# A state-space block and a bilinear feed-forward layer on one core: factor products in one visit, decays inside pair 1's wait, pairs 2, 3 and 5 reordered

## The chip, the core and the metric

The kernel runs on one core of one Trainium2 chip. A core has TensorE (PE, matrix products into the accumulation memory PSUM; PEld is its weight load), VectorE (DVE), ScalarE (ACT), GpSimd (POOL) and SyncE (SP, which only issues transfers); 16 DMA engines move data between memory and the core. ACT and POOL issue some transfers as well. The metric is the device time of one execution in microseconds; lower is better. The figure for a kernel is the median of several executions.

## The reference

Inputs: x (4 batches, 8 heads, 768 positions, 32 columns), a (4, 8, 768), B and C (4, 8, 768, 16), and three weight matrices. The first half is a recurrence with decays, computed in chunks; the second a feed-forward layer without a nonlinearity, in which two projections are multiplied.

```python
for c in range(nc):                               # chunks of 32 positions in the reference
    cum = np.cumsum(log_a[chunk])
    L = np.exp(cum[i] - cum[j]) * (i >= j)
    y_intra = (C_i . B_j * L) @ x                 # masked scores times x
    y_inter = (C_i @ state) * np.exp(cum)
    y = y_intra + y_inter
    state = exp(sum(la)) * state + sum_j B_j x_j * exp(cum[-1] - cum[j])
X = y, as 3072 tokens x 256
out = ((X @ w_a) * (X @ w_b)) @ w_out             # 256 -> 1536, 1536 -> 256, float32
```

## The kernel before, in words

**Tiles.** The kernel works in blocks of 128 positions: NBLK = 6 blocks, and in each two pairs (NBP = 2) of batches, so 12 pairs, p = 0 to 11; pair p belongs to block p // 2. Inside a pair the two batches are indexed bt. Pairs 0 to 3 (p < P0) hold positions in an even/odd layout and have their B and C turned by TensorE (`transposes`); pairs 4 to 11 have them turned by a transposing transfer from SP (`turn`). All products take float16 operands, except the factor and decay products, which are float32.

**Decays.** Running products Pr of a within each block come from VectorE (`scan`, L225), rmid is one over the product at position 63, selr spreads that over heads. A factor product (`factors_mm`, L240) turns Pr into fC, one factor for each position and head; fB is its reciprocal (`fb`). For block 1 it is written as four small products (L260), for blocks 2 to 5 as two half-width ones each (L248); each logical product appears as two records in the profile. B times fB and C times fC (`scale_bc`) give bm and cm. Three small POOL steps make hr, hs and hsx, the decay from one block to the next spread over batches, and one product (gps, L815) with the head indicator spreads it over partitions; ACT copies it to G.

**A pair.** `scores(p)` multiplies C by B into four PSUM banks SC. `mask` multiplies each of the four by the causal mask: VectorE does it directly from PSUM; with `by_pool=True` ACT first copies to tmp and POOL multiplies. `scale_x` makes X16 from x. `pv(p)` (products L433, with the state's part L477 from block 1 on, and the new state's sums L460 in `ds_mm`) makes the output of the recurrence, which ACT and VectorE evacuate to X2T, the input of the feed-forward layer. `state_sums` (VectorE) and `state_spread` (POOL) carry the state on to the pair of the next block. From block 2 on a block's two pairs share `outputs`, called by `group`.

**Feed-forward.** For pairs 0 to 3, a unit (p, k2) is 4 products with Wa, 4 with Wb (L601, 256 columns each), an ACT copy of the first result (asb, L615) and a VectorE product of the two (hk, L622); six units make a pair's hidden layer, and `out_half(p, bt)` multiplies it by Wo in 12 products (L637), which ACT evacuates (`out_store`). From block 2 on, `bunit` (L667) and `bout` (L694) do the same for a whole block. The first halves of Wa and Wb (k2 = 0, 1, 2) are loaded early, the second halves (k2 = 3, 4, 5) by `load_w(1)` from POOL.

**Order.** The schedule is manual: each engine runs its instructions in the order in which the Python text issues them, and a program adds semaphore waits. So the text is the order of every queue, SP's and POOL's too, and a POOL transfer keeps POOL busy while it is issued. The feed-forward has four PSUM banks; `bank` hands them out in the order of the string BANKS, and a product that gets a bank waits until that bank's last reader is done. Warm-up products (`warmup`, L218) multiply zeros and are read by nobody.

The lines around the change, in the order of the text: the front with pair 1 (L754 to L818), the units of pairs 0 and 1 (L836 to L842), pair 2 (L850 to L858), pair 3 (L912 to L930), pairs 4 and 5 (L931 to L951), and the last stores (L707).

Of the kernel before, what the change touches and what calls it, by code (L numbers as in the profile page):

```python
# [14 lines left out]
ALU = mybir.AluOpType  # L15
# [4 lines left out]
YS = 16.0  # L20

BANKS = (
    "01231031203120312031230123012301203120321032103120312031203213012301203210321032130120312"
    "0312032130213021302132013201320132013201320132013021302130213021302130213021302130213021"
)


# [1 line left out]
def kernel(  # L29
# [13 lines left out]
    nc = tc.nc  # L43
# [83 lines left out]
    def bank(name):  # L127
        return psf.tile([128, 512], f32, name=name, tag=f"ff{next(banks)}")
# [89 lines left out]
    def warmup(n, bank, cols=512):  # L218
        for _ in range(n):
            nc.tensor.matmul(  # L220
                bank[:, 0:cols], warm[:, 0:128], warm[:, 0:cols], start=True, stop=True, skip_group_check=True
            )
# [462 lines left out]
    def bout(blk, c, parts=1):  # L685
        bt, j = divmod(c, NBP)
        hk = st[("FF", blk)]["hk"]
        rows = out[(2 * j + bt) * S + blk * Q :][0:Q]
        w = d_model // parts
        for part in range(parts):  # L690
            o_ps = bank("ops")
            cs = slice(part * w, part * w + w)
            for k in range(NK):
                nc.tensor.matmul(  # L694
                    o_ps[:, 0:w],
                    hk[:, k, c * Q : (c + 1) * Q],
                    Wo[:, k, cs],
                    start=(k == 0),
                    stop=(k == NK - 1),
                    skip_group_check=True,  # L700
                )
            o_sb = outp.tile([128, d_model], f32, name="osb", tag="osb")
            if parts > 1 and part == 0:
                nc.vector.tensor_scalar(o_sb[:, 0:w], o_ps[:, 0:w], 1.0 / (YS * YS), None, ALU.mult)
            else:
                nc.scalar.activation(out=o_sb[:, 0:w], in_=o_ps[:, 0:w], func=AF.Copy, scale=1.0 / (YS * YS))  # L706
            (nc.sync, nc.scalar)[part].dma_start(rows[:, cs], o_sb[:, 0:w])  # L707

    def loads_bc(p):
        if p < NP:  # L710
# [11 lines left out]
    def go(*items):  # L722
        for p, k2 in items:
            unit(p, k2)()
# [47 lines left out]
    scan(5, NBLK)  # L772
    over_mid(1, NBLK)
    sel_over_mid(1, NBLK, nc.vector)
    warmup(2, tcp)
    aps = [unit_mm(0, 0, Wa), unit_mm(0, 1, Wa)]
    asb = [evac_a(aps[0])]
    scores(1)
    mask(product(1, 3), by_pool=True)
    aps.append(unit_mm(0, 2, Wa))  # L780
    asb.append(evac_a(aps[1]))
    asb.append(evac_a(aps[2]))
    fps = bank("fps")
    factors(1, 3, fps)
    scale_x(1, nc.scalar)
    for m in range(3):
        mask(product(1, m))
# [1 line left out]
    for bt in range(2):  # L789
        load1(nc.gpsimd, 2, 1, bt)  # L790
    load_wo(0)
    nc.gpsimd.tensor_copy(maskbd, headm.unsqueeze(2).broadcast_to((128, H, D)))
    nc.gpsimd.tensor_tensor(out=hr, in0=Pr[:, 0:NG, Q - 1], in1=rmid[:, 0:NG], op=ALU.mult)
    nc.gpsimd.tensor_tensor(out=hs, in0=hr, in1=Pr[:, 1:NBLK, 63], op=ALU.mult)
    nc.gpsimd.tensor_tensor(
        out=hsx,
        in0=hs.unsqueeze(1).broadcast_to((BH, nb, NG)),
        in1=selb.rearrange("p (b g) -> p b g", b=nb),
        op=ALU.mult,
    )  # L800
    load_wo(1)
    tiles(3)
    for bt in range(2):
# [1 line left out]
    times(0, 0, bps[0], asb[0])  # L805
    pv(1, DS=(0, SC[:2]), split=True)
    ds_mm(0, 64, SC[:2])
    for k2 in range(1, 3):
        times(0, k2, bps[k2], asb[k2])
    fb(1)  # L810
    scale_bc(2, 0, nc.gpsimd)
    scale_bc(2, 1, nc.gpsimd)
    go((1, 0), (1, 1), (1, 2))
    gps = bank("gps")
    nc.tensor.matmul(  # L815
        gps[:, 0 : nb * NG], indm, hsx.rearrange("p b g -> p (b g)"), start=True, stop=True, skip_group_check=True
    )
    nc.scalar.copy(G.rearrange("p b g -> p (b g)"), gps[:, 0 : nb * NG])  # L818
    factors(3, NBLK, bank("fps"))
    state_sums(0)  # L820
    state_sums(1)
    state_spread(0)
# [10 lines left out]
        load1(nc.sync, 3, 1, bt)  # L833
    loads_x(3, nc.sync)
    loads_bc(4)
    go((0, 3), (0, 4), (1, 3), (0, 5))  # L836
    transposes(2, apart=True)
    go((1, 4))
    h = unit(1, 5)
# [6 lines left out]
    scale_x(2, nc.scalar)  # L846
    scale_bc(3, 0, nc.gpsimd)
    scale_bc(3, 1, nc.gpsimd)
    scale_x(3, nc.gpsimd)
    loads_bc(5)  # L850
    o = [bank("ops"), bank("ops")]
    out_mm(0, 0, o[0], range(6))
    out_mm(0, 1, o[1], range(6))
    out_mm(0, 0, o[0], range(6, NK))
    out_store(0, 0, o[0])
    pull(2)
    pv(2, split=True)
    out_mm(0, 1, o[1], range(6, NK))  # L858
    out_store(0, 1, o[1])
    h = unit(2, 0, lambda: transposes(3, apart=True))  # L860
    state_sums(2)
    fb(2)
# [47 lines left out]

    scores(3)
    prep(4, (2,))  # L912
    loads_bc(6)
    prep(5)
    loads_x(4, nc.sync)
# [1 line left out]
    loads_bc(7)  # L917
    mask(product(3, 0))
    h()
    for m in range(1, 4):  # L920
        mask(product(3, m))
    out_half(1, 0)
    out_half(1, 1)
    go((2, 2))
    pull(3)
    pv(3)
    state_sums(3)
    fb(3)
    state_spread(3)
    go((2, 3), (2, 4), (2, 5))  # L930
    scores(4)  # L931
    mask(product(4, 3), by_pool=True, by_token=True)
    prep(6)
    masked(4, (0, 1, 2))
    out_half(2, 0)
    o_ps = bank("ops")
    out_mm(2, 1, o_ps, range(NK))
    out_store(2, 1, o_ps)
    go((3, 0))
    scores(5)  # L940
    mask(product(5, 3), by_pool=True, by_token=True)
    prep_x(4)
# [1 line left out]
    prep(7)  # L944
    loads_x(7, nc.sync)
    loads_bc(8)
    masked(5, (0, 1, 2), *pu(3, 1, 2, 3))
    go((3, 4))
    scale_x(5, nc.scalar)
    go((3, 5))  # L950
    group(2)  # L951
# [92 lines left out]
```

## Time and profile before

| | |
|---|---|
| median of 3 runs | 124.44 us (124.07 to 124.65) |
| profiled execution | 123.91 us |
| its span, first to last instruction | 122.2 us |
| granted TensorE clock | 1.000 |
| TensorE busy | 117.1 us, 96% of the span |
| VectorE, ScalarE, GpSimd busy | 85.9, 71.4, 61.9 us |
| memory read, written | 11.13, 3.15 MB |

The profile describes one execution. Its page gives busy times and shares, the span in 40 slices, the chain of work that ended last, and groups of instructions by source line; the trace can also be asked for a timeline, for who waited for whom, and for one tile's or one line's instructions. A name such as `aps<-X2T,Wa` says that the tile aps is written from X2T and Wa; "128*128 128x256" that 128 rows and 128 columns of the array are used and 128 x 256 elements written; "x4" that four neighbouring instructions are merged. A bracket at a line's end gives the idle time before it and what ended that. Matmuls are pipelined, so two neighbours overlap in the timeline, and their cost is the distance between their starts.

### The profile page before, as it was taken

How to read it: one execution, taken by the hardware profiler on the slowest of the kernel's cores; microseconds unless marked ns; L12 is line 12 of the kernel's file. 1: busy time of each engine (PE TensorE's matmuls, PEld its weight loads, DVE VectorE, ACT ScalarE, POOL GpSimd, SP SyncE). 2: the span in 40 equal slices, each digit the busy share in tenths (PEclk: the TensorE clock that was granted, in tenths of full speed). 3: DMA queues.
4: the chain of work that ended last, by engine and by line, in shares of the span. 5: the costliest groups of instructions: out<-in, count | busy, mean ns of one | idle time of the engine just before them, and what ended most of it. 6: DMA issues, size and time to landing. Idle time of an engine off the chain costs nothing.

```text
span 122.2 us, 3713 instructions
## 1 busy us (share of the span) xinstructions
PE 117.1 (96%) x1455; PEld 80.1 (66%) x1455; DVE 85.9 (70%) x163; ACT 71.4 (58%) x141; POOL 61.9 (51%) x107
## 2 busy tenths in 40 slices
PE   5999999999999999999999999999999999999990
PEld 2446789978898898644476464766465684645880
DVE  1877897795969599499984999667799435748000
ACT  0367756866466477887668637745645737575230
POOL 7999998966953876099921993147400000000000
PEclk9999999999999999999999999999999999999999
DMA  3999999998969999799789854879501012010131
GB/s 64 165 167 240 152 215 155 218 143 83 95 95 131 150 104 155 76 134 148 55 143 128 200 187 127 96 102 160 161 0 51 16 45 68 0 48 0 43 117 55
DMA packets 66737, 13.73 MB, mean 112 GB/s; under 512 B 61616, under 2 KB 66384, under 8 KB 66720
## 3 DMA queue, kind: packets, MB, share of 16 engines
q1 hardware_dynamic: 62592, 9.53, 49.8%
q0 software_dynamic: 2128, 3.61, 16.8%
q10 hardware_dynamic: 2000, 0.36, 1.6%
q8 instruction: 11, 0.18, 0.7%
q14 instruction: 6, 0.05, 0.1%
HBM read 11.13 MB, written 3.15 MB: 117 GB/s over the span
## 4 chain that ended last, share of the span: by engine, by line
PE 93%; ACT 1%; issue 1%; POOL 1%; DVE 1%; POOLq 0%
PE ops L694 18%; PE aps L667 17%; PE bps L667 17%; PE aps L601 9%; PE ops L637 9%; PE bps L601 9%; PE SC L220 3%; PE SC L358 2%; PE SC L419 2%; PE SC L373 1%; PE SC L433 1%; PE SC L508 1%; PE fps L260 1%; POOL bm L304 1%; ACT bt L337 1%
## 5 line engine op out<-in xcount | busy, mean ns | idle before, releaser
L615 ACT COPY asb<-aps 128x512 f32<-128x512 f32 x72 | 42.0, 586 | 14.3 <-PE aps L667 9.6
L679 DVE TENSOR_TENSOR hkb<-bps,asb 128x512 f16<-128x512 f32 x48 | 32.4, 689 | 12.6 <-ACT asb L615 11.4
L667 PE MATMUL aps<-XB,Wa 128*128 128x512 f16 x96 | 28.6, 379 | 0.0
L667 PE MATMUL bps<-XB,Wb 128*128 128x512 f16 x96 | 28.5, 379 | 0.0
L694 PE MATMUL ops<-Wo,hkb 128*128 128x256 f16 (+1 forms) x204 | 22.5, 267 | 0.0
L694 PEld LDWEIGHTS <-hkb 128*128 128x128 f16 x204 | 18.5, 98 | 3.1
L413 DVE TENSOR_TENSOR t<-SC,causal_q 128x512 f16<-128x512 f32 x27 | 17.3, 682 | 3.3 <-PE SC L358 3.3
L622 DVE TENSOR_TENSOR hk<-bps,asb 128x512 f16<-128x512 f32 x24 | 16.2, 684 | 4.1 <-ACT asb L615 3.7
L667 PEld LDWEIGHTS <-Wb 128*128 128x128 f16 x96 | 9.9, 103 | 10.9
L667 PEld LDWEIGHTS <-Wa 128*128 128x128 f16 x96 | 9.7, 103 | 9.1 <-issue 0.2
L601 PE MATMUL aps<-X2T,Wa 128*128 128x256 f16 x96 | 14.3, 274 | 0.2 <-DVE X2T L493 0.2
L706 ACT ACTIVATE osb<-ops 128x256 f32<-128x256 f32 (+1 forms) x16 | 6.0, 377 | 14.3 <-PE ops L694 14.2
L601 PE MATMUL bps<-X2T,Wb 128*128 128x256 f16 x96 | 14.1, 273 | 0.0
L411 POOL TENSOR_TENSOR t<-tmp,causal_q 128x512 f16<-128x512 f32 x5 | 5.8, 1161 | 11.7 <-ACT tmp L410 11.6
L289 POOL TENSOR_SCALAR x<-xn 128x512 f16<-128x512 f32 x7 | 10.4, 1490 | 2.1 <-DMA xn<-in_x_dram 1.8
L637 PE MATMUL ops<-Wo,hk 128*128 128x256 f16 x96 | 11.3, 273 | 0.0
L601 PEld LDWEIGHTS <-Wa 128*128 128x128 f16 x96 | 9.4, 103 | 1.3 <-DVE X2T L493 0.3
L601 PEld LDWEIGHTS <-Wb 128*128 128x128 f16 x96 | 9.8, 103 | 0.6
L637 PEld LDWEIGHTS <-hk 128*128 128x128 f16 x96 | 9.0, 98 | 1.3
L413 DVE TENSOR_TENSOR t<-SC,causal 128x512 f16<-128x512 f32 x13 | 8.2, 684 | 0.9 <-PE SC L373 0.8
L304 POOL TENSOR_TENSOR bm<-bn,fB 128x256 f16<-128x256 f32 x11 | 7.1, 642 | 2.5 <-DMA bn<-in_B_dram 1.7
L296 POOL TENSOR_TENSOR planes<-cn,fC 128x256 f16<-128x256 f32 x8 | 5.0, 620 | 4.7 <-DMA cn<-in_C_dram 4.5
(94 smaller groups left out, 117.0 us busy)
## 6 DMA issues: line engine op xcount, KB each, us to landing
out_dram<-osb SPq DMA_DIRECT2D x23, 128.0 KB, 1.8
xn<-in_x_dram SPq DMA_DIRECT2D x7, 256.0 KB, 4.2
cn<-in_C_dram SPq DMA_DIRECT2D x8, 128.0 KB, 3.9
bn<-in_B_dram SPq DMA_DIRECT2D x8, 128.0 KB, 4.5
Wa<-in_moe_w_a_dram POOLq DMA_DIRECT2D x2, 384.0 KB, 5.9
Wb<-in_moe_w_b_dram POOLq DMA_DIRECT2D x2, 384.0 KB, 7.3
Wo<-in_moe_w_out_dram POOLq DMA_DIRECT2D x2, 384.0 KB, 6.7
xn<-in_x_dram POOLq DMA_DIRECT2D x4, 128.0 KB, 6.5
```

Source lines behind the costliest of these rows:

```text
L289: eng.tensor_scalar(xo, xi, XS, None, ALU.mult)
L304: eng.tensor_tensor(out=m_, in0=raw, in1=(f[:, blk, :, bp] if factor is None else factor).unsqueeze(3).broadcast_to((128, 2, H, N)), op=AL ...
L411: nc.gpsimd.tensor_tensor(out=o_, in0=tmp, in1=c_, op=ALU.mult)
L413: nc.vector.tensor_tensor(out=o_, in0=i_, in1=c_, op=ALU.mult)
L601: nc.tensor.matmul(ps[:, kk * 2 * Q : (kk + 1) * 2 * Q], W[k // 6][:, f, k % 6 // 3 * 384 : (k % 6 // 3 + 1) * 384].rearrange("p (c kk) -> ...
L615: (nc.vector.tensor_copy if on_dve else nc.scalar.copy)(asb, a_ps)
L622: nc.vector.tensor_tensor(out=s["hk"][:, 2 * k2 : 2 * k2 + 2, :].rearrange("p k q -> p (k q)"), in0=b_ps, in1=asb, op=ALU.mult)
L637: nc.tensor.matmul(o_ps[:, 0:d_model], hk[:, k, bt * Q : (bt + 1) * Q], Wo[:, k, :], start=(k == 0), stop=(k == NK - 1), skip_group_check= ...
L667: nc.tensor.matmul(t_, W[k // 6][:, f, k % 6 // 3 * 384 : (k % 6 // 3 + 1) * 384].rearrange("p (c kk) -> p kk c", kk=3)[:, k % 3], XB[:, b ...
L679: return lambda: nc.vector.tensor_tensor(out=s["hk"][:, k], in0=ps[1], in1=asb, op=ALU.mult)
L694: nc.tensor.matmul(o_ps[:, 0:w], hk[:, k, c * Q : (c + 1) * Q], Wo[:, k, cs], start=(k == 0), stop=(k == NK - 1), skip_group_check=True,)
L706: nc.scalar.activation(out=o_sb[:, 0:w], in_=o_ps[:, 0:w], func=AF.Copy, scale=1.0 / (YS * YS))
```

## The change

- Two warm-up products ahead of unit (0, 0) are dropped.
- The POOL steps hr, hs and hsx are issued ahead of pair 1's pooled mask, instead of after the first Wo load and maskbd.
- `factors` makes blocks 1 to 5 in one visit ahead of pair 0's Wb products (24 records and one copy), instead of blocks 1 and 2 there and blocks 3 to 5 after unit (1, 2).
- gps moves from after unit (1, 2) to after pair 1's `pv` and pair 0's `ds_mm`, and becomes two products of 64 columns of the array each.
- Units (0, 3), (0, 4), (1, 3): the three Wa halves with their copies first, then the three Wb halves.
- Pair 2: the second half of `out_half(0, 1)` and the first 6 products of `out_half(1, 0)` go ahead of `pv(2)`, the other 6 behind it.
- Pair 3: its fourth mask goes by ACT and POOL instead of VectorE; `scale_x(3)` goes from POOL to ACT; unit (2, 3) comes ahead of `pv(3)`; `out_half(1, 0)` is no longer here.
- Pairs 4 and 5: units (3, 1) and (3, 2) come ahead of `scores(5)`, and `out_half(2, 1)` behind pair 5's masks.
- The store of the last column group of block 4 is issued by POOL instead of SP.
- BANKS is another string, one shorter.

```diff
@@ -20,8 +20,8 @@
 BANKS = (
-    "01231031203120312031230123012301203120321032103120312031203213012301203210321032130120312"
...
+    "0123102310231012301230123012031230123013201320130213021302130213021320312031203102132013"
...
@@ -704,7 +704,8 @@
                 nc.vector.tensor_scalar(o_sb[:, 0:w], o_ps[:, 0:w], 1.0 / (YS * YS), None, ALU.mult)
             else:
                 nc.scalar.activation(out=o_sb[:, 0:w], in_=o_ps[:, 0:w], func=AF.Copy, scale=1.0 / (YS * YS))
-            (nc.sync, nc.scalar)[part].dma_start(rows[:, cs], o_sb[:, 0:w])
+            eng = nc.gpsimd if (blk, c) == (NBLK - 2, 3) else (nc.sync, nc.scalar)[part]
+            eng.dma_start(rows[:, cs], o_sb[:, 0:w])
 
     def loads_bc(p):
         if p < NP:
@@ -772,16 +773,23 @@
     scan(5, NBLK)
     over_mid(1, NBLK)
     sel_over_mid(1, NBLK, nc.vector)
-    warmup(2, tcp)
     aps = [unit_mm(0, 0, Wa), unit_mm(0, 1, Wa)]
     asb = [evac_a(aps[0])]
+    nc.gpsimd.tensor_tensor(out=hr, in0=Pr[:, 0:NG, Q - 1], in1=rmid[:, 0:NG], op=ALU.mult)
+    nc.gpsimd.tensor_tensor(out=hs, in0=hr, in1=Pr[:, 1:NBLK, 63], op=ALU.mult)
+    nc.gpsimd.tensor_tensor(
+        out=hsx,
+        in0=hs.unsqueeze(1).broadcast_to((BH, nb, NG)),
+        in1=selb.rearrange("p (b g) -> p b g", b=nb),
+        op=ALU.mult,
+    )
     scores(1)
     mask(product(1, 3), by_pool=True)
     aps.append(unit_mm(0, 2, Wa))
     asb.append(evac_a(aps[1]))
     asb.append(evac_a(aps[2]))
     fps = bank("fps")
-    factors(1, 3, fps)
+    factors(1, NBLK, fps)
     scale_x(1, nc.scalar)
     for m in range(3):
         mask(product(1, m))
@@ -790,14 +798,6 @@
         load1(nc.gpsimd, 2, 1, bt)
     load_wo(0)
     nc.gpsimd.tensor_copy(maskbd, headm.unsqueeze(2).broadcast_to((128, H, D)))
-    nc.gpsimd.tensor_tensor(out=hr, in0=Pr[:, 0:NG, Q - 1], in1=rmid[:, 0:NG], op=ALU.mult)
-    nc.gpsimd.tensor_tensor(out=hs, in0=hr, in1=Pr[:, 1:NBLK, 63], op=ALU.mult)
-    nc.gpsimd.tensor_tensor(
-        out=hsx,
-        in0=hs.unsqueeze(1).broadcast_to((BH, nb, NG)),
-        in1=selb.rearrange("p (b g) -> p b g", b=nb),
-        op=ALU.mult,
-    )
     load_wo(1)
     tiles(3)
     for bt in range(2):
@@ -805,18 +805,24 @@
     times(0, 0, bps[0], asb[0])
     pv(1, DS=(0, SC[:2]), split=True)
     ds_mm(0, 64, SC[:2])
+    gps = bank("gps")
+    for c0 in (0, 64):
+        nc.tensor.matmul(
+            gps[c0 : c0 + 64, 0 : nb * NG],
+            indm[:, c0 : c0 + 64],
+            hsx.rearrange("p b g -> p (b g)"),
+            start=True,
+            stop=True,
+            skip_group_check=True,
+            tile_position=(0, c0),
+        )
+    nc.scalar.copy(G.rearrange("p b g -> p (b g)"), gps[:, 0 : nb * NG])
     for k2 in range(1, 3):
         times(0, k2, bps[k2], asb[k2])
     fb(1)
     scale_bc(2, 0, nc.gpsimd)
     scale_bc(2, 1, nc.gpsimd)
     go((1, 0), (1, 1), (1, 2))
-    gps = bank("gps")
-    nc.tensor.matmul(
-        gps[:, 0 : nb * NG], indm, hsx.rearrange("p b g -> p (b g)"), start=True, stop=True, skip_group_check=True
-    )
-    nc.scalar.copy(G.rearrange("p b g -> p (b g)"), gps[:, 0 : nb * NG])
-    factors(3, NBLK, bank("fps"))
     state_sums(0)
     state_sums(1)
     state_spread(0)
@@ -833,7 +839,11 @@
         load1(nc.sync, 3, 1, bt)
     loads_x(3, nc.sync)
     loads_bc(4)
-    go((0, 3), (0, 4), (1, 3), (0, 5))
+    us = [(0, 3), (0, 4), (1, 3)]
+    asb = [evac_a(unit_mm(p, k2, Wa)) for p, k2 in us]
+    for (p, k2), a_ in zip(us, asb):
+        times(p, k2, unit_mm(p, k2, Wb), a_)
+    go((0, 5))
     transposes(2, apart=True)
     go((1, 4))
     h = unit(1, 5)
@@ -846,17 +856,20 @@
     scale_x(2, nc.scalar)
     scale_bc(3, 0, nc.gpsimd)
     scale_bc(3, 1, nc.gpsimd)
-    scale_x(3, nc.gpsimd)
     loads_bc(5)
     o = [bank("ops"), bank("ops")]
     out_mm(0, 0, o[0], range(6))
     out_mm(0, 1, o[1], range(6))
     out_mm(0, 0, o[0], range(6, NK))
     out_store(0, 0, o[0])
+    out_mm(0, 1, o[1], range(6, NK))
+    out_store(0, 1, o[1])
+    o_ps = bank("ops")
+    out_mm(1, 0, o_ps, range(6))
     pull(2)
     pv(2, split=True)
-    out_mm(0, 1, o[1], range(6, NK))
-    out_store(0, 1, o[1])
+    out_mm(1, 0, o_ps, range(6, NK))
+    out_store(1, 0, o_ps)
     h = unit(2, 0, lambda: transposes(3, apart=True))
     state_sums(2)
     fb(2)
@@ -910,6 +923,7 @@
 
     scores(3)
     prep(4, (2,))
+    mask(product(3, 3), by_pool=True)
     loads_bc(6)
     prep(5)
     loads_x(4, nc.sync)
@@ -917,26 +931,23 @@
     loads_bc(7)
     mask(product(3, 0))
     h()
-    for m in range(1, 4):
+    for m in range(1, 3):
         mask(product(3, m))
-    out_half(1, 0)
+    scale_x(3, nc.scalar)
     out_half(1, 1)
-    go((2, 2))
+    go((2, 2), (2, 3))
     pull(3)
     pv(3)
     state_sums(3)
     fb(3)
     state_spread(3)
-    go((2, 3), (2, 4), (2, 5))
+    go((2, 4), (2, 5))
     scores(4)
     mask(product(4, 3), by_pool=True, by_token=True)
     prep(6)
     masked(4, (0, 1, 2))
     out_half(2, 0)
-    o_ps = bank("ops")
-    out_mm(2, 1, o_ps, range(NK))
-    out_store(2, 1, o_ps)
-    go((3, 0))
+    go((3, 0), (3, 1), (3, 2))
     scores(5)
     mask(product(5, 3), by_pool=True, by_token=True)
     prep_x(4)
@@ -944,8 +955,9 @@
     prep(7)
     loads_x(7, nc.sync)
     loads_bc(8)
-    masked(5, (0, 1, 2), *pu(3, 1, 2, 3))
-    go((3, 4))
+    masked(5, (0, 1, 2))
+    out_half(2, 1)
+    go((3, 3), (3, 4))
     scale_x(5, nc.scalar)
     go((3, 5))
     group(2)
```

More of the change, by code (lines that the diff above doesn't have):

```diff
@@ L22 @@
 BANKS = (
-    "01231031203120312031230123012301203120321032103120312031203213012301203210321032130120312"
-    "0312032130213021302132013201320132013201320132013021302130213021302130213021302130213021"
+    "0123102310231012301230123012031230123013201320130213021302130213021320312031203102132013"
+    "2013203102310231023103210321032103210321032103210231023102310231023102310231023102310231"
 )
```

## The prediction

> **What bounds the kernel now.** I read the page first (who is busy, at what clock, what the chain consists of), then TensorE's waits, then the timeline of 8 to 20 us and of 24 to 48 us, where the edits lie.
>
> ```profile
> PE 117.1 (96%) x1455; PEld 80.1 (66%) x1455; DVE 85.9 (70%) x163; ACT 71.4 (58%) x141; POOL 61.9 (51%) x107
> ...
> PEclk9999999999999999999999999999999999999999
> ...
> PE 93%; ACT 1%; issue 1%; POOL 1%; DVE 1%; POOLq 0%
> ```
>
> TensorE (PE) is the chain, at full clock in every slice. The waits view of PE has one row for the start and these two:
>
> ```profile
> PE SC L373 <- ACT bt L337: 0.2, 1, 0.2
> PE aps L601 <- DVE X2T L493: 0.2, 1, 0.2
> ```
>
> So after 16 us PE waits for nobody that the view shows: a change wins only by taking instructions or switches out of PE's queue, and loses wherever it makes PE wait. The timeline of the edited stretch (start, duration, engine, line, count):
>
> ```profile
> 10.49 0.59 PE L220 MATMUL tc<-warm 128*128 128x512 f16 x2
> ...
> 10.92 1.04 PE L601 MATMUL aps<-X2T,Wa 128*128 128x256 f16 x8
> ...
> 11.60 1.44 POOL L148 DMA_DIRECT2D bn<-in_B_dram  x2
> ...
> 12.79 0.42 PE L260 MATMUL fps<-selr,Pr 32*64 32x16 f32 x8
> ...
> 13.06 0.28 PE L248 MATMUL fps<-selr,Pr 32*64 32x32 f32 x4
> 13.11 1.16 POOL L411 TENSOR_TENSOR t<-tmp,causal 128x512 f16<-128x512 f32 x1
> 13.27 1.49 PE L601 MATMUL bps<-X2T,Wb 128*128 128x256 f16 x12
> ...
> 14.70 0.42 PE L433 MATMUL SC<-t,x 64*32 64x128 f16 x32
> ...
> 14.95 0.59 PE L460 MATMUL SC<-x,bm 64*32 64x64 f16 x32
> ...
> 15.22 0.42 DVE L493 TENSOR_SCALAR X2T<-SC 128x256 f16<-128x256 f32 x1 [0.28 <-PE SC L433]
> ...
> 15.70 0.62 PE L601 MATMUL aps<-X2T,Wa 128*128 128x256 f16 x4 [0.16 <-DVE X2T L493]
> ...
> 16.69 0.22 POOL L793 TENSOR_TENSOR hr<-Pr,rmid 32x5 f32<-32x5 f32 x1
> ...
> 17.50 0.79 POOL L170 DMA_DIRECT2D Wo<-in_moe_w_out_dram  x1
> ...
> 17.91 0.60 PE L601 MATMUL bps<-X2T,Wb 128*128 128x256 f16 x4
> ...
> 18.44 0.39 PE L815 MATMUL gps<-hsx,c 32*128 32x20 f32 x2
> ...
> 18.76 0.54 PE L248 MATMUL fps<-selr,Pr 32*64 32x32 f32 x12
> ...
> 19.23 0.62 PE L601 MATMUL aps<-X2T,Wa 128*128 128x256 f16 x4
> ```
>
> Durations of products overlap, so I price PE by starts: two 512-column warm-ups take 10.92 - 10.49 = 0.43; eight 256-column products 0.87, so 0.109 each and 0.44 for a half unit of four.
>
> **The change part by part.**
>
> *Two warm-ups gone.* The products behind them read X2T, whose last evacuation ends at 10.46, and can start at 10.49: everything on PE is 0.43 earlier. Scores of pair 1 move from 11.88 to 11.45; their first half needs bt's first copy (ends 11.16) and ct (11.14), so nothing new is late there.
>
> *All factors in one visit.* Twelve more small records go behind the first twelve. Twelve cost 0.47 (18.76 to 19.23), four cost 0.21 (13.06 to 13.27), switch back included: 0.033 each by the difference, and 0.029 if the switch costs what it does elsewhere (0.15); I take 0.37 for twelve. Their inputs are there: VectorE's last scan, reciprocal and selr end by 11.99. The Wb products start at 13.27 - 0.43 + 0.37 = 13.21, pair 1's pv could start at 14.64. One copy of 160 columns replaces two on ScalarE (0.24 each); it costs nothing on the path, since x(1) behind it was done at 14.65 and ScalarE's row starts earlier.
>
> *The three small POOL steps ahead of pair 1's pooled mask.* POOL is in the two bn issues until 11.60 + 1.44 = 13.04, later than everything that hr reads. The three steps took 17.50 - 16.69 = 0.81 with their hand-overs. The mask therefore starts at 13.85 and ends at 15.01; with 0.04 for the hand-over PE sees it at 15.05. Heads 6 and 7 need it, the last 12 of pv's 32 products; in the trace these began at about 14.70 + 20/32 x 0.25 = 14.86. So pv ends 0.19 later than before: the mask that was off the path (done at 14.27) becomes the gate, and takes back all that the warm-ups gave. Queued behind it on POOL: two cn issues and the first Wo issue 0.8 later. cn's landing is behind Wb's in the same queue anyway; Wo's two landed 6.6 to 6.8 after issue, so at 23.0 and 24.3, and the output products that read the halves come at 24.5 and 25.8: covered. The second xn issue already waited for Wb until 19.32, which absorbs the shift, so bm(2) stays at 20.02.
>
> *The decays' product (gps) in pair 1's wait.* The ds products end at 15.54 in the trace and PE then waits for X2T, which is read at 15.70; without that wait it would have gone on at about 15.48 (at 28.07 the output products start 0.06 before the modelled end of such a ds group). So 0.22 is free. The two half-width products, two passes each, are of the form 32*64: about 0.06 as two pairs of factor records. Bounds: nothing if the 0.22 hides all, the whole 0.32 of the old place (18.44 to 18.76) if nothing is hidden. Between 64*32 and 32*64 there may be a switch; the nearest row is gps to factors, 0.13 behind the second gps start plus its own 0.06, so 0.19. 0.19 + 0.06 - 0.22 leaves 0.03, and I take 0.05. The Trainium skill (TensorEngine Tiling (Array Packing), Key Properties) says that a change of tiling mode, not of tile, drains the array; this case's rows agree (0.20 between starts on entering a tiled form, 0.15 on leaving). It speaks against this place, since the old one had gps and factors share one way in and out; by it the sum below would be 0.05 smaller than for a gps wholly hidden.
>
> *The second visit gone.* The next half unit after 17.91 would start at 18.35; it starts at 19.23. That removes 0.88.
>
> *Three Wa half units, then three Wb.* The same 24 products. By the steps so far the first starts at 19.23 - 0.88 + 0.19 + 0.05 = 18.59; the first that reads the second half of Wb comes at 19.90 instead of 19.03. SP's load that waits for this Wb goes out at 19.09, so the old order would have gained a wait. New neighbours: the first Wb product takes the bank of (1,2)'s, free at 19.42 + 0.24 = 19.66; (0,5) at 21.21 takes that of the third Wa, which ScalarE copies at 0.59 each by about 20.95. Both hold by a quarter of a us: nothing, at most 0.2 if the copies run late. G's copy is ahead of the asb copies in a gap of 0.75 on ScalarE: nothing.
>
> *Pair 2.* Twelve output products move ahead of pv(2): 1.31 more cover. The 18 products before pv(2) at 25.16 should end at 27.13, and the next start is 27.25, when VectorE's masks end (27.19): 0.10 gained. The same 12 are missing later, so order alone moves scores(3) by +1.31, pv(3) by 0.87, scores(4) by 0.
>
> *Pair 3.* Mask (3,3) leaves VectorE (0.63) for ScalarE (0.59) and POOL (1.16); x(3) leaves POOL (1.50, and a 1.04 wait before it) for ScalarE (0.63). Cover between scores and pv falls from 32 products to 28, 0.44 less, but VectorE has 0.63 less: nothing. POOL: pair 4's steps can start when cn(4) lands, so by about 29.8 instead of 30.95, and end with gU(2) near 33.0; the mask takes it to 34.2, and planes(5) and bm(5) (0.62 each) end at 35.4, where the trace has 35.44. So pair 5's transposing load keeps its time.
>
> *Pair 5.* Scores(5) come four products later in the order. In the trace the load was issued at 36.25 and took 5.4 to land, so 41.65; scores(5) move from 42.17 to 42.17 + 0.44 - 0.74 = 41.87. Covered by 0.2. Masks then have 36 instead of 40 products before the group, and are first in VectorE's queue: nothing. x(4) ends on POOL near 45.7, read at 46.5.
>
> *One store on POOL.* SP issued each late store as it came and has nothing to queue behind. POOL's loads landed 3 to 8 us after issue against SP's 1.7; issued at 113.3 it lands at 121.4 at worst, with the last store at 120.1 then; nearest, with DMA idle 90%, are the short ones. Nothing, bound +1.3.
>
> **Sum** against the profiled execution, 123.91 us (span 122.2 and 1.7 around it): -0.88 + 0.19 + 0.05 - 0.10 = -0.74, so 123.17. That execution lies 0.53 under the median of the three runs, 124.44 (124.07 to 124.65); against the median the forecast is 123.70, 0.6% faster. About 0.5% is what a measurement of this kernel tells from no change.
>
> **Rivals.**
> 1. The POOL mask is no gate (its three steps run quicker between other work). Then pv starts at 14.64 and gps hides: -0.06 - 0.88 - 0.10 = -1.04, 123.4. For: the steps work on 5 to 20 columns. Against: their 0.81 in the trace.
> 2. Given back in small waits: gps at 0.32 and 0.2 for a bank in the Wa-Wb run: -0.74 + 0.27 + 0.2 = -0.27, 124.2, no change. For: margins of 0.2. Against: ScalarE and VectorE keep pace at the same rate as before.
> 3. Slower, by one mechanism: the transposing load of pair 5 lands late, because POOL has mask (3,3) ahead of pair 5's steps, SP waits for POOL, and x(4) queues behind. PE then waits one for one past 41.87. With the whole 1.16 added it lands at 42.8 and 0.9 comes back: 124.6. It is slower by over 0.5% from a landing 1.6 late (43.3) on; at 1.8 late, 125.3. For: this landing was the longest of the eight (2.8 to 5.4). Against: POOL sheds x(3) first, and bm(5) had stood idle 0.78.
>
> **How the numbers follow.** Forecast 0.47, rival 1 0.12, rival 2 0.24, rival 3 0.17. Four fifths of the forecast lie beyond 0.5% (under 123.82): faster 0.38 + 0.12 = 0.50; same 0.09 + 0.24 = 0.33; slower 0.17. The range goes from rival 1 less half the runs' spread (0.29), 123.1, to 124.9, just past rival 3's milder case; the forecast's own is 123.4 to 124.0.
>
> **What would show it.** Right: no warm-up at 10.5, one factor visit with 24 records, POOL's mask ending near 15.0 with PE's pv held for POOL, gps between ds and (1,0), Wa of (0,3) at about 18.6, scores(4) near 37.5, all later stages 0.7 earlier. Wrong: PE waits for POOL much before or after 15.05, a wait for ScalarE or VectorE at 19 to 24, or PE held at scores(5).

## The result and the profile after

The changed kernel takes 123.0 us (median of four, 122.51 to 123.35) against 124.25 (124.02 to 124.65) for the kernel before on the same chip: ratio 0.9885 [0.9849, 0.9921]. Two later comparisons gave 0.989 [0.9846, 0.9934] and 0.9908 [0.9887, 0.9928]. The forecast was 123.70 us, 0.6% faster, with a range of 123.1 to 124.9. The direction was right; the gain is nearly twice the forecast, and the median lies just under the range.

The profiled execution took 122.51 us, its span 120.81 (before: 123.91 and 122.21), so the 1.40 us lies wholly inside the span. Busy times and the chain, from the page of the changed kernel:

```profile
PE 115.7 (96%) x1455; PEld 79.4 (66%) x1455; DVE 85.2 (71%) x162; ACT 72.1 (60%) x142; POOL 62.3 (52%) x108
...
PEclk9999999999999999999999999999999999999999
...
PE 89%; DMA 4%; POOL 3%; issue 0%; ACT 0%; POOLq 0%
```

TensorE still carries the chain at full clock, but a transfer has entered it with 4%: the load of Wa's first half. The waits view of PE has three rows for the changed kernel, all of them before 12 us.

The timeline of the changed kernel where most of the edits lie:

```profile
10.58 0.78 PEld L601 LDWEIGHTS <-Wa 128*128 128x128 f16 x8 [0.31 <-DMA Wa<-in_moe_w_a_dram]
10.58 1.06 PE L601 MATMUL aps<-X2T,Wa 128*128 128x256 f16 x8
...
12.48 0.42 PE L260 MATMUL fps<-selr,Pr 32*64 32x16 f32 x8
...
12.74 0.63 PE L248 MATMUL fps<-selr,Pr 32*64 32x32 f32 x16
12.78 0.25 POOL L778 TENSOR_TENSOR hr<-Pr,rmid 32x5 f32<-32x5 f32 x1
...
13.31 1.49 PE L601 MATMUL bps<-X2T,Wb 128*128 128x256 f16 x12
...
13.55 1.16 POOL L411 TENSOR_TENSOR t<-tmp,causal 128x512 f16<-128x512 f32 x1
...
14.03 0.63 ACT L287 ACTIVATE x<-xn 128x512 f16<-128x512 f32 x1
...
14.73 0.42 PE L433 MATMUL SC<-t,x 64*32 64x128 f16 x32
...
15.55 0.29 PE L810 MATMUL gps<-hsx,c 32*64 32x20 f32 x4
...
15.77 0.62 PE L601 MATMUL aps<-X2T,Wa 128*128 128x256 f16 x4
...
17.98 0.60 PE L601 MATMUL bps<-X2T,Wb 128*128 128x256 f16 x4
...
18.41 1.47 PE L601 MATMUL aps<-X2T,Wa 128*128 128x256 f16 x12
```

Set against the rows of before, this is where the time went, by starts on PE, and in the last three rows by landings and ends:

| mark | before | after | moved |
|---|---|---|---|
| first Wa product | 10.92 | 10.58 | -0.34 |
| first factor record | 12.79 | 12.48 | -0.31 |
| first Wb product | 13.27 | 13.31 | +0.04 |
| pair 1's pv | 14.70 | 14.73 | +0.03 |
| unit (1, 0) | 15.70 | 15.77 | +0.07 |
| unit (0, 3) | 19.23 | 18.41 | -0.82 |
| transposes of pair 2 | 22.74 | 21.91 | -0.83 |
| scores(4) | 38.24 | 37.28 | -0.96 |
| last product | 118.70 | 117.75 | -0.95 |
| last landing of a transfer | 120.85 | 119.90 | -0.95 |
| SP's last wait is over | 121.30 | 119.91 | -1.39 |
| end of the span | 122.21 | 120.81 | -1.40 |

Two gains, then: 0.95 us on TensorE, all of it made by 38 us, and 0.44 us after the last landing, where no engine computes. SP's waits after 117 us, first before and then after, show the second (waited-for, then us in total, times, longest):

```profile
SPq L1039 <- DMA out_dram<-osb: 1.8, 1, 1.8
```

```profile
SPq L1051 <- DMA out_dram<-osb: 1.4, 3, 0.7
```

Before, SP sat 1.8 us on one transfer and then still had a list to go through. After, it is done 0.01 us behind the last landing.

### The profile page after: what moved, and what is told of

Read it like the earlier page. It is cut to its first block, busy times and chain, and to the rows that moved or that the text cites. A ratio compares the mean times of both kernels' runs of the same rounds, so it can differ in the third digit from the quotient of the medians.

```text
span 120.8 us, 3711 instructions
## 1 busy us (share of the span) xinstructions
PE 115.7 (96%) x1455; PEld 79.4 (66%) x1455; DVE 85.2 (71%) x162; ACT 72.1 (60%) x142; POOL 62.3 (52%) x108
## 4 chain that ended last, share of the span: by engine, by line
PE 89%; DMA 4%; POOL 3%; issue 0%; ACT 0%; POOLq 0%
PE ops L694 18%; PE aps L667 18%; PE bps L667 17%; PE ops L637 9%; PE aps L601 9%; PE bps L601 9%; DMA Wa<-in_moe_w_a_dram 4%; PE SC L358 2%; PE SC L419 2%; POOL cn L148 1%; PE SC L373 1%; PE SC L433 1%; PE SC L508 1%; POOL bn L148 1%; POOL causal L208 1%; PE SC L460 1%
## 5 line engine op out<-in xcount | busy, mean ns | idle before, releaser
L615 ACT COPY asb<-aps 128x512 f32<-128x512 f32 x72 | 41.8, 586 | 14.1 <-PE aps L667 9.7
L708 POOL DMA_DIRECT2D out_dram<-osb x1 | 0.6, 639 | 27.3 <-ACT osb L706 27.3
L289 POOL TENSOR_SCALAR x<-xn 128x512 f16<-128x512 f32 x6 | 8.9, 1489 | 1.0 <-DMA xn<-in_x_dram 0.7
```

The lines of the kernel that those rows point to most:

```text
L289: eng.tensor_scalar(xo, xi, XS, None, ALU.mult)
```

## The experiments

Two theories were to be told apart from rivals. **A (the end):** at the end SP waits for the semaphores of all transfers one after the other, in a fixed order, and the one store that POOL issues shifts which semaphore the last store reports to; the 0.44 us is the rest of the list behind it. Its rival: the store's own landing or the queue's load counts. **L (the front):** pair 1's pv starts when x(1) or the Wb products are ready, x(1) is set by the landing of xn(1), and so the warm-ups and the factors ahead of it are cheap either way. Its rivals: the warm-ups' 0.43 us or POOL's mask count, as the prediction had it.

### The end of the program

**One store back on SP**, the rest of the change kept:

```diff
-            eng = nc.gpsimd if (blk, c) == (NBLK - 2, 3) else (nc.sync, nc.scalar)[part]
-            eng.dma_start(rows[:, cs], o_sb[:, 0:w])
+            (nc.sync, nc.scalar)[part].dma_start(rows[:, cs], o_sb[:, 0:w])
```

> The changed kernel with one part undone: block 4's last store goes out on SP again. Theory A (the end of the program): SP waits for the semaphores of all transfers one after the other, about 0.06 us each, and the SP and ACT transfers take eight semaphores in turn. In the kernel before, the last store's semaphore was waited for second, so seven waits stood behind the last landing (120.85 to 121.32 in its trace); in the changed kernel it is the last one waited for (119.90 to 119.94). With the store on SP the turn falls back: about 0.4 us comes back between the last landing and the end, TensorE unchanged, 123.4 us against the changed kernel's 123.0. Theory B (the prediction's: that store costs and brings nothing): no difference, the whole gain lies on TensorE, 123.0.

The ratio to the kernel before was 0.997 [0.9941, 1.0] (124.18 against 124.45): slower than both theories had it. Its trace shows two things. The tail is back: last landing 121.01, SP's last wait over at 121.45, 0.44 us. And its front was late for reasons that the store cannot have: Wa landed at 11.05 (10.54 in the changed kernel's profile), xn(1) at 14.61 (13.94), and the transposes of pair 2 waited 0.46 us for another late tile. So this run confirmed A's size in the trace and left the time open; it was repeated below.

**The kernel before with that one store on POOL**, and with **another store of the same block** instead:

```diff
+            eng = nc.gpsimd if (blk, c) == (NBLK - 2, 3) else (nc.sync, nc.scalar)[part]
```

```diff
+            eng = nc.gpsimd if (blk, c) == (NBLK - 2, 0) else (nc.sync, nc.scalar)[part]
```

> The kernel before with that one store on POOL and nothing else. Theory A: TensorE unchanged, the end 0.4 us sooner after the last landing, 123.85 against 124.25. Theory B: no difference, 124.25.

> The kernel before with another store on POOL: block 4's first column group, some 20 us before the end, and the last one on SP as before. Theory A (only the turn of the semaphores counts): the same 0.4 us as with the late store, 123.85. A rival to it (the late store itself is relieved, SP's queue at the end being one shorter): no difference, 124.25.

0.9966 [0.9935, 0.9997] and 0.997 [0.9944, 0.9996]: 0.34% and 0.30% of 124.45, about 0.4 us each, with nothing else changed in the kernel; each interval only just leaves out no change. Which of the two stores goes to POOL does not matter. SP's waits after 117 us show the same row in both:

```profile
SPq L1040 <- DMA out_dram<-osb: 1.4, 3, 0.7
```

**All stores of block 4 on POOL**, in the kernel before:

```diff
+            eng = nc.gpsimd if blk == NBLK - 2 else (nc.sync, nc.scalar)[part]
```

> The kernel before with all four stores of block 4 on POOL. Theory A: the turn moves by four places, so three waits stand behind the last landing, about 0.2 us between the last landing and SP's last wait, where the kernel before has 0.45 and one store on POOL has 0.04. The rival (fewer SP stores near the end are better): less than with one store on POOL.

One execution, 123.64 us; the tail is 0.20 us, between the two others. This is the run that best separates A from its rival, because more stores off SP did not make the end shorter still. The trace gives the semaphore of every transfer and SP's last waits, nine of them, issued by the line that calls the kernel, about 0.06 us each when nothing is left to wait for. Transfers from SP and ACT take eight semaphores in turn, waited for at the 2nd to the 9th place; POOL's take others. One transfer less in that turn puts the last store one place back in it, from the 2nd round to the 9th; four less put it at the 6th:

| kernel | last landing | SP's last wait over | between | last store's place in the nine waits |
|---|---|---|---|---|
| before | 120.85 | 121.30 | 0.45 | 2nd, seven behind it |
| changed, store on SP | 121.01 | 121.45 | 0.44 | 2nd |
| before, four stores on POOL | 120.83 | 121.03 | 0.20 | 6th, three behind it |
| before, one store on POOL | 121.72 | 121.73 | 0.01 | 9th, none behind it |
| changed | 119.90 | 119.91 | 0.01 | 9th |

**Store back on SP, timed again** beside the changed kernel:

> The changed kernel with block 4's last store on SP, once more. If the store is worth only the end of the program: 0.35% slower than the changed kernel beside it, whatever the landings. If the first figure (0.3% faster than before) was right as it stood: 0.8% slower than the changed kernel, and there would be something that the traces have not shown.

> The changed kernel beside the next three, on one chip: 1.1% faster than before, as in two comparisons; if landings are late on this chip (first Wa after 11.0, second half of xn(1) after 14.4), less, about 0.7%, since its front waits for them where the kernel before waits less.

0.9944 [0.9919, 0.997] (123.41 us) without the store on POOL, 0.9908 [0.9887, 0.9928] (122.93 us) with it: 0.36%, 0.45 us, though the two intervals overlap a little; the trace has the same 0.44 (120.55 to 120.99). The changed kernel's 0.92% lies between the two figures expected of it; in its trace the landings were early (Wa 10.18, xn(1) 13.63), so it does not show what late ones cost. In the profiled execution with the store on SP Wa came late (11.22), and PE shows that it waits one for one:

```profile
11.27 1.06 PE L601 MATMUL aps<-X2T,Wa 128*128 128x256 f16 x8 [0.74 <-DMA Wa<-in_moe_w_a_dram]
```

A is shown by its size in every trace above and by the in-between case, which it orders rightly. The times agree with it in three comparisons (0.30 to 0.36%), none of them far clear of its noise; the first comparison of the store on SP gave 0.85% and does not fit by time. A kernel further below that moves two loads from POOL to ACT adds to it: two transfers more in the turn, the last store at the 3rd place, 0.39 us behind its landing.

### The front

**The two warm-ups put back**, then once more with more executions:

```diff
+    warmup(2, tcp)
     aps = [unit_mm(0, 0, Wa), unit_mm(0, 1, Wa)]
```

> The changed kernel with the two warm-ups back. Theory L (landings): pair 1's pv cannot start sooner than 0.76 after the second half of xn(1) has landed, because ACT scales x(1) first (seven traces so far: landings from 13.71 to 14.81, pv 0.76 to 0.82 behind where it waits for x), nor sooner than 1.42 after the first Wb product. The warm-ups take 0.43 of a time in which TensorE otherwise waits for Wa, so the first Wa product starts at the later of 10.7 and Wa's landing, and pv at the later of 14.85 and the landing of xn(1) plus 0.76: 0 to 0.13 behind the changed kernel. The prediction's theory (the pooled mask is the gate, the warm-ups' 0.43 is taken back whole): no difference. A theory in which the warm-ups' 0.43 counts: 0.43 later.

> The changed kernel with the two warm-ups back, once more. Theory L (the front is set by the landings of Wa and xn(1)): 0 to 0.1% slower than the changed kernel, not to be told apart. If the warm-ups' 0.43 us counted: 0.35% slower.

The first gave 123.13 us in one execution, with pv at 14.84, 0.11 later than in the changed kernel, and a wait of 0.5 us that neither theory has, in pair 0's state sums (PE at L460, put down to "issue"). Its cause stays open. The second gave 0.9894 [0.9875, 0.9912] (122.82 us), not to be told from the changed kernel beside it (0.9908). In its trace Wa's products started at 10.85, as late as the warm-ups make them, and unit (0, 3) at 18.61, 0.2 later than in the changed kernel (18.41, and 18.42 beside it). Dropping the warm-ups is worth between nothing and 0.2 us, not 0.43.

**POOL's three small steps issued twice**, so that the pooled mask of pair 1 comes later still:

```diff
         op=ALU.mult,
     )
+    nc.gpsimd.tensor_tensor(out=hr, in0=Pr[:, 0:NG, Q - 1], in1=rmid[:, 0:NG], op=ALU.mult)
+    nc.gpsimd.tensor_tensor(out=hs, in0=hr, in1=Pr[:, 1:NBLK, 63], op=ALU.mult)
+    nc.gpsimd.tensor_tensor(
+        out=hsx,
...
+    )
     scores(1)
```

> The changed kernel with the three small POOL steps done twice ahead of the pooled mask, the second time over the first with the same values: 0.8 us more on POOL. In the changed kernel's trace the mask ends at 14.71 and its heads' products come at 14.89, or later where pv waits for x(1), so it has 0.15 of room or more. The mask ends at about 15.5 now: pv of pair 1 starts as before, but ends 0.4 to 0.65 later, and so does everything behind it. If the mask were already the gate: 0.8 later. If it had much room: nothing.

123.96 us in one execution, with a late front. Its timeline:

```profile
14.80 1.15 POOL L411 TENSOR_TENSOR t<-tmp,causal 128x512 f16<-128x512 f32 x1
...
15.03 0.63 ACT L287 ACTIVATE x<-xn 128x512 f16<-128x512 f32 x1 [0.75 <-DMA xn<-in_x_dram]
...
15.71 0.57 PE L433 MATMUL SC<-t,x 64*32 64x128 f16 x32 [0.52 <-ACT x L287]
```

The mask now ended at 15.94, and the last pv products waited for it: pv to the state sums took 0.36 instead of 0.25 us. That is 0.11, not the 0.4 to 0.65 expected, because x(1) ended only at 15.66 (xn(1) had landed at 14.95) and held pv's start meanwhile. The mask can be a gate, as the prediction modelled it; x(1) is another, and the later one counts.

The mask was a gate, if a small one, in two executions of the changed kernel itself. In its two repeats, one reported above and one below, it ended at 14.78 and 14.90 (14.70 in the first trace), and the last 12 products of pv started 0.05 behind it, at 14.84 and 14.95. From pv to the state sums it took 0.30 and 0.29 us instead of 0.25. The later of the two:

```profile
13.75 1.15 POOL L411 TENSOR_TENSOR t<-tmp,causal 128x512 f16<-128x512 f32 x1
...
14.74 0.51 PE L433 MATMUL SC<-t,x 64*32 64x128 f16 x32
```

**The changed kernel again, and a kernel that brings Wa forward.** In the second, two small loads of pair 1's C go to ACT's queue, and two loads of pair 2 come later, so that POOL reaches Wa sooner:

```diff
+    load1(nc.scalar, 1, 1, 0)
+    load1(nc.scalar, 1, 1, 1)
...
-    load1(nc.gpsimd, 1, 1, 0)
-    load1(nc.gpsimd, 1, 1, 1)
     load_w(0)
...
-    for bt in range(2):
-        load1(nc.gpsimd, 2, 0, bt)
...
     mask(product(1, 3), by_pool=True)
+    for bt in range(2):
+        load1(nc.gpsimd, 2, 0, bt)
```

> The changed kernel once more, beside the kernel before, for a narrower figure. The undone store measured 0.3% faster than the kernel before, so with 0.43 us (0.35%) of the program's end added theory A expects 0.65% faster, 123.65 us against 124.45. If the first comparison (1.15%) stands, something besides TensorE's queue and the end of the program counts. In the trace: TensorE's first Wa product starts when the first half of Wa has landed (10.54 in the first trace, 11.05 to 11.44 in the three timed experiments since), not when the transposes are done.

> The changed kernel, with pair 1's two cn loads issued by ACT instead of POOL, so that POOL issues the first Wa about 1.4 us sooner, and with pair 2's two bn loads issued behind the pooled mask instead of ahead of the three small steps. Theory W (the landing of Wa is what the dropped warm-ups uncovered): Wa lands before 10.2, the first Wa product starts at about 10.3 instead of 10.6 or later, and everything behind is 0.2 to 0.5 us sooner: 123.2 us where the changed kernel has 123.6. The prediction's theory (the pooled mask is the gate, whatever is ahead of it): the mask is now 1.4 us sooner as well, so 0.2 is won at most. Rival: the DMA engines were busy all the time anyway, Wa lands only 0.2 sooner and pair 1's cn later, no gain.

The repeat gave 0.989, as above, so the first comparison stands. The other kernel was slower than before, 1.0374 [1.031, 1.0438] (129.53 us), although Wa did land at 9.82. The expectation that the DMA engines would be too busy for it came nearest, but it had no gain, and the runs show a loss. What lost were small loads beside it: pair 1's B, issued by SP at 3.82 as in the changed kernel, landed at 13.54 (8.43 there), and ACT's two loads of C at 13.9 to 14.1. That they lost by sharing the DMA engines with Wa and Wb is the likely reading; no run separates it from the other moves of this edit. PE waited for them:

```profile
13.70 0.62 POOL L304 TENSOR_TENSOR bm<-bn,fB 128x256 f16<-128x256 f32 x1 [3.98 <-DMA bn<-in_B_dram]
...
14.37 0.35 PE L326 MATMUL SC<-ident,bm 128*128 128x128 f16 x2 [3.07 <-POOL bm L304]
```

And it paid twice. By stretches of the span (us; busy PE, PEld, DVE, ACT, POOL; then the granted clock, the DMA share and GB/s):

```profile
11.00:14.40 3.40, 0.33 (x17) 0.13 (x3) 0.21 (x1) 0.28 (x1) 0.70 (x2) 1.00 0.67 122
14.40:17.90 3.50, 3.50 (x48) 2.20 (x48) 2.37 (x8) 1.87 (x4) 2.03 (x5) 0.51 0.63 69
17.90:21.00 3.10, 3.10 (x103) 2.55 (x101) 2.28 (x5) 2.07 (x6) 2.88 (x4) 1.00 1.05 188
```

After the idle 3 us the granted clock was 0.51 for the next 3.5 us, and products of 256 columns came 0.213 us apart instead of 0.109. The Trainium skill (TensorE: Matmul & The Clock Gate, Part 1: The HAM clock gate) says that the clock falls to half after an idle window of about 3.4 us and returns after about as long a busy one. The row agrees with the return. The fall came sooner than the page has it, behind an idle stretch of 3.07 us by PE's own row.

Over all the runs, the landings move while the work behind them does not: Wa's first half landed between 10.16 and 11.44, and xn(1) between 13.63 and 14.95. Where xn(1) came late, pv started 0.76 to 0.77 behind its landing: 14.61 to 15.37, 14.81 to 15.57, 14.50 to 15.27, 14.52 to 15.28, 14.95 to 15.71, and 13.85 to 14.61 in the repeat of the changed kernel. L is shown as far as that goes: what sets pv's start is the later of xn(1) + 0.76 and the first Wb product + 1.42. In the first trace of the changed kernel these are 14.70 and 14.73, so there it was TensorE's own queue, by a hair. Why a landing moves by 1.3 us between executions of one order of issue was not found.

### The visits, decays and pairs

**Blocks 3 to 5 back in a second factor visit:**

```diff
-    factors(1, NBLK, fps)
+    factors(1, 3, fps)
...
     go((1, 0), (1, 1), (1, 2))
+    factors(3, NBLK, bank("fps"))
```

> The changed kernel with the factors in two visits again (blocks 1 and 2 first, blocks 3 to 5 behind unit (1, 2)); the decay product stays in pair 1's wait. Switches have a price: the second visit costs 0.10 on entering, 0.35 for its records, 0.10 on leaving, 0.56 from the half unit before it to the one behind it, and 0.35 is saved in the first visit, so from the first factor product to the first Wa product of unit (0, 3) it takes 0.2 longer than in the changed kernel (5.93 there, 12.48 to 18.41). If only the records cost: no difference.

**The decays' product back in its old place**, at full width:

```diff
-    gps = bank("gps")
-    for c0 in (0, 64):
-        nc.tensor.matmul(
...
     go((1, 0), (1, 1), (1, 2))
+    gps = bank("gps")
+    nc.tensor.matmul(
+        gps[:, 0 : nb * NG], indm, hsx.rearrange("p b g -> p (b g)"), start=True, stop=True, skip_group_check=True
+    )
+    nc.scalar.copy(G.rearrange("p b g -> p (b g)"), gps[:, 0 : nb * NG])
```

> The changed kernel with the decay product at its old place behind unit (1, 2), full width; the factors stay in one visit. It is then a visit by itself: 0.10 on entering, 0.25 for its two passes, 0.12 on leaving, and 0.05 is won back in pair 1's wait. From the first factor product to the first Wa product of unit (0, 3) about 0.4 longer than the 5.93 of the changed kernel. If the product hid nothing in that wait: 0.1 or less.

These two had late landings at the front, so they are read by distances on PE, not by their times (123.61 and 123.48 us in one execution each). The extra visits, first of the factors alone and then of the decays alone:

```profile
19.01 0.54 PE L248 MATMUL fps<-selr,Pr 32*64 32x32 f32 x12
```

```profile
19.02 0.39 PE L815 MATMUL gps<-hsx,c 32*128 32x20 f32 x2
```

From (1, 0) to (0, 3) the changed kernel takes 2.64 us, which is just its six half units. With the factor visit it takes 3.21, so that visit costs 0.57; with the decays it takes 3.05, so that one costs 0.41. The first visit gets 0.35 shorter without its twelve extra records (0.48 instead of 0.83), which makes one visit worth 0.22 net (0.2 was expected). From pair 0's state sums to unit (1, 0) it took 0.76 us without the decays and 0.79 with them, so they cost 0.03 there (nothing in the last repeat of the changed kernel, 0.75), and the move is worth nearly 0.4, as expected. Each visit alone, the two add up to 0.98; side by side in the kernel before they cost 0.88, so they shared 0.1 of the way in and out. That agrees with the Trainium skill (TensorEngine Tiling (Array Packing), Key Properties), which has TensorE drain when the tiling mode changes, not when the tile does. Apart, the two visits change the form four times (into 32*128 and back, into 32*64 and back); side by side they change it three times.

**Pairs 2, 3 and 5 in the old order**, then again with more executions; the core of the edit is pair 2's:

```diff
-    out_mm(0, 1, o[1], range(6, NK))
-    out_store(0, 1, o[1])
-    o_ps = bank("ops")
-    out_mm(1, 0, o_ps, range(6))
     pull(2)
     pv(2, split=True)
-    out_mm(1, 0, o_ps, range(6, NK))
-    out_store(1, 0, o_ps)
+    out_mm(0, 1, o[1], range(6, NK))
+    out_store(0, 1, o[1])
...
```

> The changed kernel with the reorders of pairs 2, 3 and 5 undone (from pair 2's transposes to group 2 as in the kernel before). From the first Wa product of unit (0, 3) to scores(4) the changed kernel takes 18.87 us, the kernel before 19.01. Theory: the only gain of the reorders is TensorE's wait for VectorE's masks ahead of pv(2), 0.10 to 0.14, so 18.97 to 19.01. Rival (with the front sooner by 0.8, the old order now waits for the later loads, xn(2) and pair 5's turned tile): 19.2 or more, and more than 0.2 between scores(4) and group 2.

> The changed kernel with the reorders of pairs 2, 3 and 5 undone, once more. TensorE's wait ahead of pv(2) alone: 0.1 to 0.34 us, 0.1 to 0.3% slower than the changed kernel. Rival (the old order also waits for late loads): 0.5% or more.

The first execution (123.50 us) was confused by a late landing of pair 2's C (0.45 us of wait). The timed one gave 0.9932 [0.9907, 0.9957], 123.29 us, against 0.9908 for the changed kernel beside it: 0.3 us, with intervals that overlap. Its trace has a loss of the same size: from the transposes of pair 2 to scores(4) it takes 15.71 us, the changed kernel 15.37, the kernel before 15.50; from scores(4) to group(2) 8.76 against 8.74, so pair 5's order is worth nothing. Where the 0.34 lies, from its timeline:

```profile
27.04 0.63 ACT L287 ACTIVATE x<-xn 128x512 f16<-128x512 f32 x1 [1.14 <-DMA xn<-in_x_dram]
27.20 0.38 PE L477 MATMUL SC<-ct,sbd 128*128 128x128 f16 x4
...
27.72 0.42 PE L433 MATMUL SC<-t,x 64*32 64x128 f16 x32
```

From the transposes to the state's products (L477) it takes 4.51 us, as in the kernel before; the changed kernel needs 4.39 without the twelve output products that it moved there. So 0.12 is the wait for VectorE's masks, near the forecast 0.10. The other 0.2 lies between L477 and pv(2), 0.52 us instead of 0.32: pv(2) waited for x(2), and that for xn(2), which landed at 27.02.

This second wait is not shown to be a price of the old order. PE was no sooner in this execution than in the kernel before (unit (0, 3) at 19.20 against 19.23); the landing was later, 27.02 against 25.80, and 25.68 to 26.19 in the three traces of the changed kernel. An estimate from these rows: with the changed kernel's early front the old order would have pv(2) ready at 26.73, x(2) lets it start 0.70 behind xn(2)'s landing, and so it would lose between nothing and 0.16 us beside the 0.12. The twelve output products that moved ahead of pv(2) cover that in the changed kernel.

**Wa and Wb halves by turns, as before:**

```diff
-    us = [(0, 3), (0, 4), (1, 3)]
-    asb = [evac_a(unit_mm(p, k2, Wa)) for p, k2 in us]
-    for (p, k2), a_ in zip(us, asb):
-        times(p, k2, unit_mm(p, k2, Wb), a_)
-    go((0, 5))
+    go((0, 3), (0, 4), (1, 3), (0, 5))
```

> The changed kernel with units (0, 3), (0, 4), (1, 3) in the old order, Wa and Wb half in turn. The second half of Wb landed between 18.35 and 19.69 in the traces so far; the first product that reads it would come 0.44 after the first Wa product of (0, 3), at about 18.85, where the changed kernel has it at 19.72. So a wait of 0 to 0.8, the landing of Wb less 18.8, and from (0, 3) to the transposes of pair 2 3.55 plus that wait (3.55 in the changed kernel without a wait). If the order is free: 3.55 whatever the landing.

123.66 us in one execution; from (0, 3) to the transposes of pair 2 it took 3.80 us instead of 3.50. Neither expectation holds as put: the wait is there, but Wb's second half had landed by about 19.1, ahead of the first product that reads it (19.43). The stall is at unit (1, 3):

```profile
19.98 0.85 DVE L563 TENSOR_SCALAR U<-SC,G 128x64 f32<-128x64 f32 x4
20.75 1.28 DVE L622 TENSOR_TENSOR hk<-bps,asb 128x512 f16<-128x512 f32 x2
21.48 0.60 PE L601 MATMUL bps<-X2T,Wb 128*128 128x256 f16 x4
```

The last product above starts at 21.48, where 21.17 was its turn: it needs a bank that VectorE's hk still reads, and hk stood behind the four state products U. U started 0.99 us behind unit (0, 3) here and 0.10 behind it in the kernel before (19.33 and 19.23). The removed visit used to give VectorE this time; with it gone, the order Wa, Wa, Wa, Wb, Wb, Wb gives it back.

One rival is untested. The stall belongs to the old order together with its hand-out of banks: this run kept the string BANKS of the changed kernel, which gives that product the bank of (0, 3)'s Wb half, as the string of the kernel before does. The bank of (0, 4)'s Wa half was free at 21.09, when ScalarE's copy of it ended. Another string might have spared the old order the wait.

## Why the prediction was right, and where it failed

The time fell below the range, and two terms of the sum are to blame: the store on POOL, put at nothing, and POOL's mask, put at +0.19.

- **Second visit gone, -0.88: right.** From the last Wb product of (1, 2) to (0, 3) it was 1.32 us, now 0.43: -0.89.
- **Warm-ups, -0.43, and twelve more factor records, +0.37: the records' price right, the warm-ups' gain not.** The records cost 0.35. But Wa's products came only 0.34 earlier, as Wa landed at 10.54; the prediction had looked at X2T alone. The two cancel at the first Wb product (13.31 against 13.27; the prediction had 13.21). Put back, the warm-ups cost between nothing and 0.2 us.
- **POOL's mask as a gate, +0.19: failed in size.** The mask ended at 14.70, 14.78 and 14.90 in the three traces of the changed kernel (forecast 15.01). In the first of them that was ahead of the products that read it, at 14.85, and PE did not wait for POOL; in the others it held the last 12 products of pv and cost 0.05 and 0.04. Unit (1, 0) started at 15.77, 15.77 and 15.78, 0.07 or 0.08 later than before, where the forecast, with the decays, had 0.24. The step that failed is that POOL's row was moved by the new steps and by nothing else. The three steps took 0.77 us (12.78 to 13.55), near the forecast 0.81, but in the first trace POOL came out of its bn issues at 12.80 instead of 13.04, as pair 0's mask had started 0.18 sooner. Nor did pv start at 14.64: Wb's products held it until 14.73, and x(1), done at 14.66, was about as late.
- **Decays in pair 1's wait, +0.05: right**, +0.04 at most. **Pair 2, -0.10: right**, -0.13 down to scores(4).
- **Wa and Wb order "nothing": right for the change, wrong as a reason.** In one execution with the old order a stall of 0.3 us came that the removed visit had hidden; the prediction looked for it at Wb's landing, and it is at VectorE.
- **Pairs 3 and 5, nothing: right.** Pair 5's transposed tile landed at 41.15 instead of 41.61, so rival 3 did not come about; rival 2's small waits did not either.
- **One store on POOL, "Nothing, bound +1.3": failed, and the larger miss.** It is -0.44 us in the traces, and three comparisons agree. The prediction looked at when the store lands, and bounded on one side only; the end of the program, from the last landing to SP's last wait, was in no row that it read.

The sum by the same terms: -0.89 + 0.03 + 0.04 - 0.13 = -0.95 on TensorE, against -0.74 forecast, and -0.44 behind it; with rounding that is the 1.40 of the span. Rival 1 had -1.04 for TensorE, with the mask no gate; that is the nearer case, though not by its route, since pv did not start earlier.

## What to carry to other kernels

Work taken away ahead of a gate is worth only the slack up to that gate, so list all that a waiting product reads, with each one's landing, before one of them is called the bound. A stall that is not there now may come once the work that hid it is gone: with one visit removed, a reordering that was forecast at nothing kept 0.3 us in the one execution that undid it. And read the profile past the last product, to the last wait of the program: there the order of semaphores was worth almost half as much as everything gained on TensorE.

## What the runs showed of the hardware that was not expected

- At the end SP goes through nine waits in a fixed order, about 0.06 us each; with the last store's semaphore at the second place, 0.44 to 0.45 us follow its landing, at the sixth 0.20, and at the ninth 0.01.
- The same load lands at times up to 1.3 us apart in executions that issue it in the same order (Wa 10.16 to 11.44, xn(1) 13.63 to 14.95).
- A small load from SP took 9.7 us to land (4.6 in the changed kernel) with POOL's large loads brought forward beside it, in one trace.
- An idle stretch of PE of about 3.1 us was enough to halve the granted clock (0.51) for the next 3.5 us, in one trace.
